# A list schedule that charges TensorE's changes of width, with new plan numbers, in a fused attention and MLP kernel

## Chip, cores and metric

The kernel runs on one core of a Trainium2 chip. What counts is the device time of one execution in microseconds (us).

## The reference

Clustered attention is followed by two MLPs. Queries and keys (2 batches, 8 heads, 768 positions, 64 wide) are each assigned to the nearest of 16 centroids per head, and a query attends to the keys of its own cluster alone. The attention's output, 1536 tokens of 512, goes through two MLPs of 512 to 2048 to 512.

```python
q_assign = np.argmax(np.einsum('bhsd,hcd->bhsc', q_n, c_n), axis=-1)
k_assign = np.argmax(np.einsum('bhsd,hcd->bhsc', k_n, c_n), axis=-1)
mask = q_assign[:, :, :, None] == k_assign[:, :, None, :]
scores = np.where(mask, scale * np.matmul(q, k.transpose(0, 1, 3, 2)), -1000000000.0)
attn = softmax(scores)
x = np.matmul(attn, v)
h = x @ w_in;  x = (h * np.clip(h + 3.0, 0.0, 6.0) / 6.0) @ w_out
h = x @ w_in2; out = softplus(h) @ w_out2
```

(softmax, softplus and the two weight names of the second MLP are written short here.)

## The kernel before, in words

The attention is cut into six blocks (two batches b, three stretches u of 256 queries) of eight heads. For each head and each 128 queries, `chunk` makes the scores in PSUM (L1053), takes the row maximum on VectorE (L1056), the exponential on ScalarE (L1064) and one over the row's sum (L1066 on GpSimd or VectorE, L1068 on VectorE). In the first blocks the weights are transposed by TensorE in fp32 against a diagonal `dg` (L1089) into the one PSUM tile of pool `ps_s3`, and copied to `pt` by VectorE (L1091, four chunks) or ScalarE (L1093). In the others they are split into a high and a low fp16 part (`split`, L544 and L552) and transposed by DMA (L1097). `attend` (L1161 in fp32, L1165 in fp16) multiplies them with v. A head is 64 wide, so these products use half of TensorE's columns; two heads of a pair alternate between the two halves. For one pair that is 36 fp16 products of half width, 18 pairs in all, 648 products. All other fp16 products have the full 128 columns.

Each head's scores need K in two copies: `kb`, and `ka` with 64 rows of K and 16 rows that carry the mask. `prep` (L1018 to L1025) fills ka's lower rows from kb by ScalarE or by DMA, as the plan's `kac` says for each head.

At the start `centroids` (L814 to L850) loads the centroids, transposes them (`c0`, L821), works out their norms on VectorE (L831 to L839), spreads them (`rn`, L844, 16 copies), and transposes the normalised ones (`ct`, L846; copied to `cs`, L850). `first_matrix` (L794 to L806) prepares a matrix for the first mask on GpSimd and VectorE. `assign` multiplies q and k with the centroids (L913), scales on ScalarE, transposes (`at`, L919), and finds the best cluster (L922, L924). For the second batch the assignment products have 32 columns to move (`asc`, L905), twelve to each of four pairs of heads. One-column products (`ams`, L529) add sums over partitions.

The first MLP's products (L735 to L737) run beside the attention from the second block on; the second MLP uses Strassen's scheme (L1465 to L1467, L1630 to L1632). Every fp16 value is a pair (high, low), so three products stand for one.

The order of the work is not the order of the code. The program is first written down in the order of the due times in the table `K`. Then `own_order` builds a graph of all instructions, and `list_schedule` places them, engine by engine, by estimated durations (`estimate`), buffers that come free, and a rank; `justify` goes back from the end and gives new ranks, `K['fb']` times. The resulting order of each engine, of SyncE's DMA issues and of the buffers' turns is then imposed. The planner takes, for an engine, the instruction of best rank among those that can start within `look` ns of the earliest:

```python
            for k in r:
                s = max(free[e], at[k], floor)
...
                if s > least + look:
                    continue
```

Before, `look` is 0 for every engine. For TensorE the planner also keeps its own count of how busy the engine was, and stretches the products when it finds too little (`cold`).

Of the kernel before, what the change touches and what calls it, by code (L numbers as in the profile page):

```python
# [8 lines left out]
F32 = mybir.dt.float32  # L9
# [17 lines left out]
    'qx': -1,  # L27
    'f1': [0],
    'back': 10000,
    'look': {'PE': 0, 'Activation': 0},  # L30
    'pcp': 1,
    'r0p': [1, 2, 3, 4],
    'a0': [-0.829, -0.096, 0.131, 0.512],
    'v0': 0.183,
    'v1': 3.01,
    'a1': [2.168, 2.078, 2.929, 3.267],
    'i': [0.453, 0.631, 0.978, 1.067],
    'il': [0.349, 0.406, 0.323, 0.208],
    'o': [1.182, 1.511, 1.585, 1.881],
    'ol': [0.179, 0.317, 0.272, 0.097],  # L40
    'wd': 0.09,
    'm': [1.41, 2.61, 3.59, 4.703, 6.383],
    'ml': [0.98, 0.767, 1.125, 0.758, 1.25],
    'gq': 3,
    'gr': 1,
    'ahead': 2,
    'lag0': 0.033,
    'lag': 0.23,
    'pl': {},
    'ohb': 2,  # L50
    'gv': 2,
    'gk': [3, 0],
    'gi': [-1, -1, -1],
    'lead': 0,
    'w2o': [1.318, 1.319],
    'ly': [1.051],
    'p4': [0.046, 0.483],
    'p5': [0.833, 0.364],
    'o1': [1.321, 1.068],
    'w2': [0, 0.547, -0.309, 0.875],  # L60
    's2': [6, 13],
    'ly2': [4],
    'mo': [2, 0, 3, 1],
    'P': '',
    'qs': '',
    'x0': [2, 2, 2],
    'f0': [0, 1],
    'ze': [0],
    'w2e': [4.39],
    'w2l': 0.257,  # L70
    'tg': (),
    'we': [(1,), (0,), (0,), (0,)],
    'sb': (2, 2),
    'w2d': 0.176,
    't3': 3.736,
    'w2s': 'left',
    'te': [1, 0, 1, 0, 0, 0, 0, 0, 1, 0, 1, 0, 0, 0, 0, 0],
    'dgb': 2,
    'v2': -1.826,
    'dge': 0,  # L80
    'pg': 1,
    'pk': 1,
# [4 lines left out]
    'qdb': 1,  # L87
    'kbe': [1, 1, 1, 1],
    'dl': 200,
    'fb': 4,  # L90
    'kac': [3, 0],
    'pl_': 100,
    'w2oe': ['dve', 'dve'],
}
P14 = 2.0 ** -14
P26 = 2.0 ** -26
MASK = 2.0 ** 100
# [27 lines left out]
def estimate(op, eng, ins, outs, inst, psum):  # L125
# [8 lines left out]
    if eng == "PE":  # L134
        cols, f32 = elements(ins[0]), str(ins[0].dtype)
        m = inst.tile_size[1]
        if f32 == "dt.float32":
            t = max(cols * m / 76.8, 1.75 * m) + (90 if cols > 256 else 45 if cols > 128 else 5 if m == 128 else 40 if m == 64 else 27)
        else:
            t = cols / 2.4 + (15 if "32r" in f32 else 2.5)  # L140
            if m < 128:
                t = t / 2 + 5
        return t, t + K['pl_'], False
    if eng == "DVE":
        fast = not any(psum(a) for a in ins) and n > 8 and not getattr(inst, "is_scalar_tensor_tensor", False)
        if n <= 4:
            t = 145
        elif op == "Memset":
            t = 100 + n / 1.92
        elif op in ("TensorScalarPtr", "TensorCopy") and fast:  # L150
            t = 150 + n / 1.92
        else:
            t = 146 + n / 0.96
# [3 lines left out]
    if eng == "Activation":  # L157
        if op == "LoadActFuncSet":
            return 1200, 1330, False
        t = 200 + n / 1.2 + 85 * sum(elements(a) == 1 for a in ins[1:]) - (40 if any(psum(a) for a in ins) else 0) + (90 if len(outs) > 1 else 0)  # L160
        return t - 100, t + 30, False
    if eng == "Pool":
        if op == "TensorTensor":
            t = 170 + n * 2.15
        elif op in ("TensorScalarPtr", "TensorCopy"):
            t = 190 + n * 0.9 if n > 8 else 200
        else:
            t = 120 + n * 0.85
# [11 lines left out]
def graph(nc):  # L180
    insts = [i for i in nc.cur_bb.bb.instructions if not type(i).__name__.startswith("BassTile") and i.opcode != "RegisterMove"]
    N = len(insts)
    E = [str(i.engine).split(".")[1] for i in insts]
# [4 lines left out]
    after = [[] for _ in range(N)]  # L188
    needs = [0] * N
# [20 lines left out]
    for k, i in enumerate(insts):  # L210
# [6 lines left out]
        for a in ins + outs:  # L217
            t = a.bass_ap.tensor
            if type(t).__name__ != "Tile" or "DRAM" in str(t.space):
                continue  # L220
            if t.name not in users:
                users[t.name] = []
                g = str(t.cap_key)
# [33 lines left out]
        for x, full in before.items():  # L257
            after[x].append((k, full))
            needs[k] += 1

    g = Graph()
    g.insts, g.E, g.T, g.stream, g.cold, g.tiles, g.after, g.needs = insts, E, T, stream, cold, tiles, after, needs
    g.users, g.group, g.order, g.bufs, g.pool = users, group, order, bufs, pool
    return g


def list_schedule(g, slack, rank=None):
# [5 lines left out]
    N = len(E)  # L273
# [15 lines left out]
    at = [0.0] * N  # L289
    free = dict.fromkeys(ready, 0.0)  # L290
    port = {"DVE": 0.0, "Pool": 0.0}
    queue = 0.0
    edge, work, cold = WINDOW, 0.0, True
    for k in range(N):
        if not needs[k]:
            ready[E[k]].add(k)
# [22 lines left out]
    for _ in range(N):  # L319
        best = None  # L320
        for e, r in ready.items():
            floor = queue - K["back"] if e == "SP" else 0.0
            shared = port["Pool" if e == "DVE" else "DVE"] if e in port else 0.0
            look = K["look"].get(e, 0)
            own, least = [], 1e12
            for k in r:
                s = max(free[e], at[k], floor)
                if T[k][2]:
                    s = max(s, shared)
                if s > least + look:  # L330
                    continue
                w = gate(k)
                if w is None:
                    continue
                s = max(s, w)
                least = min(least, s)
                own.append((k, s))
            if own:
                own = min((max(s, least + look), rank[k], s, k) for k, s in own if s <= least + look)
                if best is None or own[2:] < best:  # L340
                    best = own[2:]
        s, k = best
        e = E[k]
        ready[e].discard(k)
        hold, done, shared = T[k]
        if e == "PE":
            while s >= edge:
                cold, work, edge = work < 0.41 * WINDOW, 0.0, edge + WINDOW
            work += stream[k]
            if cold:  # L350
                hold += g.cold[k]
                done = hold + K['pl_']
# [126 lines left out]
def kernel(ctx: ExitStack, tc: tile.TileContext, qT, kT, v, cen, w1i, w1o, w2i, w2o, out):  # L479
# [333 lines left out]
    def centroids():  # L813
# [28 lines left out]
        for p in range(NP):  # L842
            for r in range(4):
                nc.vector.tensor_copy(out=rn0[32 * r:32 * r + 32, p:p + 1], in_=rn[32 * p:32 * p + 32])  # L844
        ct = ps_a.tile([128, 128], F32, tag="a", name="ct")
        nc.tensor.transpose(out=ct, in_=cd.rearrange("p a d -> p (a d)"), identity=ident)  # L846
        ctv = ct.rearrange("p (n a c) -> p n a c", a=2, c=C)
        for half in range(2):
# [903 lines left out]
```

## Time and profile before

| | |
|---|---|
| median of 3 runs | 745.56 us (744.51 to 746.04) |
| the profiled execution | 746.33 us |
| its span, first to last instruction | 744.5 us |
| TensorE busy | 712.8 us (96%), 6178 records |
| VectorE busy | 614.8 us (83%) |
| ScalarE busy | 545.6 us (73%) |
| GpSimd busy | 103.8 us (14%) |
| mean granted TensorE clock | 0.991 |

The span lies within the execution's time; some 1.8 us are around it. Busy time counts every stretch in which at least one instruction of the engine ran. Matmuls are pipelined, so the distance of two starts says more than the duration of one. An fp32 product leaves two records. In the rows, PE is TensorE, DVE VectorE, ACT ScalarE, POOL GpSimd, SPq SyncE's queue of DMA issues.

### The profile page before, as it was taken

The page shows a single profiled execution, that of the slowest core. Times are in us where ns is not written, and L with a number is a line of the kernel's source. Part 1 is how long each engine was busy: PE and PEld are TensorE (multiplying, and loading weights), DVE is VectorE, ACT ScalarE, POOL GpSimd, SP SyncE. Part 2 cuts the span into 40 slices and gives each one's busy share as a digit, 9 for nine tenths or more (in the row PEclk, how much of TensorE's full clock was granted, in tenths as well). Part 3 has the DMA queues.
Part 4 walks back from the last instruction along what each step waited for, and adds up shares of the span by engine and source line. Part 5 has one row for each costly group of instructions (what it writes and reads, how often), then busy time and mean ns, then how long its engine had stood idle before and what let it go on. Part 6 is the DMA issues. An engine that isn't in the chain of part 4 may idle for free.

```text
span 744.5 us, 15777 instructions
## 1 busy us (share of the span) xinstructions
PE 712.8 (96%) x6178; PEld 592.1 (80%) x6178; DVE 614.8 (83%) x1119; ACT 545.6 (73%) x917; POOL 103.8 (14%) x170
## 2 busy tenths in 40 slices
PE   4998989999899999999999999999999999999997
PEld 1466666777688888888888888888889888888886
DVE  5599898999988868888999884999997999947930
ACT  1379789989799969987988873666886478537831
POOL 6023634311412400011012000000000000000000
PEclk8999999999999899999999999999999999999999
DMA  9394535789999958799998976044332000110001
GB/s 182 105 273 139 198 112 153 171 174 219 247 198 176 157 103 160 133 185 190 189 199 174 194 153 160 29 138 125 122 123 77 15 15 2 57 44 15 1 16 43
DMA packets 167482, 96.15 MB, mean 129 GB/s; under 512 B 129568, under 2 KB 154096, under 8 KB 167408
## 3 DMA queue, kind: packets, MB, share of 16 engines
q1 hardware_dynamic: 167408, 95.15, 55.6%
q8 instruction: 48, 0.79, 0.4%
q14 instruction: 26, 0.21, 0.1%
HBM read 54.95 MB, written 7.86 MB: 84 GB/s over the span
## 4 chain that ended last, share of the span: by engine, by line
PE 64%; DVE 19%; ACT 8%; DMA 3%; issue 3%; POOL 1%; SPq 0%; ACTq 0%; POOLq 0%; DVEq 0%
PE s L1053 6%; PE avt L1165 4%; PE h L1467 4%; PE h L1466 4%; PE h L1465 4%; PE y L735 4%; PE y L737 4%; PE y L736 4%; PE h L735 3%; PE h L736 3%; PE h L737 3%; DVE w L552 3%; PE o L1630 3%; PE o L1631 3%; PE o L1632 3%
## 5 line engine op out<-in xcount | busy, mean ns | idle before, releaser
L1056 DVE TENSOR_REDUCE nm<-s 128x1 f32<-128x768 f32 x96 | 91.2, 953 | 27.9 <-PE s L1053 26.6
L737 PE MATMUL y<-g,w 128*128 128x256 f16 x384 | 105.9, 276 | 0.9 <-DVE w L552 0.8
L735 PE MATMUL y<-g,w 128*128 128x256 f16 x384 | 105.9, 276 | 0.5 <-ACT ys L1248 0.5
L736 PE MATMUL y<-g,w 128*128 128x256 f16 x384 | 105.9, 276 | 0.0
L736 PE MATMUL h<-x,w 128*128 128x256 f16 x384 | 104.8, 273 | 0.9 <-DVE x L552 0.9
L735 PE MATMUL h<-x,w 128*128 128x256 f16 x384 | 104.7, 273 | 0.5 <-ACT pt L1093 0.3
L737 PE MATMUL h<-x,w 128*128 128x256 f16 x384 | 104.7, 273 | 0.0
L1064 ACT ACTIVATE e<-s,nm 128x768 f32<-128x768 f32 x96 | 85.9, 895 | 23.3 <-DVE r L1068 5.0
L1466 PE MATMUL h<-y,w 128*128 128x256 f16 x336 | 90.8, 273 | 0.0
L1465 PE MATMUL h<-y,w 128*128 128x256 f16 x336 | 90.3, 272 | 0.3 <-ACT y L544 0.3
L1467 PE MATMUL h<-y,w 128*128 128x256 f16 x336 | 90.3, 273 | 0.0
L735 PEld LDWEIGHTS <-w 128*128 128x128 f16 x768 | 75.9, 99 | 17.6 <-issue 7.4
L737 PEld LDWEIGHTS <-w 128*128 128x128 f16 x768 | 75.9, 99 | 14.4 <-issue 4.2
L736 PEld LDWEIGHTS <-w 128*128 128x128 f16 x768 | 76.0, 99 | 13.3 <-issue 4.3
L552 DVE SCALAR_TENSOR_TENSOR hl<-e,r,hl 128x768 f16<-128x768 f32 x72 | 74.0, 1032 | 3.3 <-ACT hl L544 2.6
L544 ACT ACTIVATE hl<-e,r 128x768 f16<-128x768 f32 x72 | 66.4, 927 | 3.6 <-DMA pt<-hl 2.2
L552 DVE SCALAR_TENSOR_TENSOR g<-a,sg,g 128x512 f16<-128x512 f32 x72 | 52.2, 759 | 9.0 <-ACT g L544 9.0
L544 ACT ACTIVATE g<-a,sg 128x512 f16<-128x512 f32 x72 | 49.0, 714 | 7.0 <-DVE a L1525 5.5
L1053 PE MATMUL s<-kb,qa 128*128 128x384 f32 x160 | 49.8, 385 | 3.7 <-ACT e L1064 3.7
L1066 POOL TENSOR_SCALAR r<-sm 128x1 f32<-128x1 f32 x64 | 24.8, 388 | 166.8 <-ACT e L1064 165.5
L1089 PEld LDWEIGHTS tr<-dg,e 128*128 128x128 f32 x288 | 35.0, 191 | 16.2 <-issue 10.8
L1228 ACT ACTIVATE r<-h,three,c 128x512 f32<-128x512 f32 x48 | 37.0, 771 | 12.8 <-PE h L737 11.5
(246 smaller groups left out, 1755.7 us busy)
## 6 DMA issues: line engine op xcount, KB each, us to landing
raw<-in_moe_w_out_dram SPq DMA_DIRECT2D x32, 512.0 KB, 3.9
raw<-in_moe_w_in_dram SPq DMA_DIRECT2D x8, 1024.0 KB, 5.2
raw<-in_moe_w_in_dram SPq DMA_DIRECT2D x16, 512.0 KB, 4.8
rk<-in_k_dram SPq DMA_DIRECT2D x12, 384.0 KB, 3.9
ka<-kb SPq DMA_DIRECT2D x20, 192.0 KB, 3.2
st<-in_v_dram SPq DMA_DIRECT2D x12, 256.0 KB, 4.2
ydram<-ys SPq DMA_DIRECT2D x12, 256.0 KB, 2.4
yl<-ydram SPq DMA_DIRECT2D x6, 512.0 KB, 3.9
```

What stands on the lines that cost most here:

```text
L544: nc.scalar.activation(out=hi, in_=src, func=ACTF.Copy, scale=scale)
L552: nc.vector.scalar_tensor_tensor(out=lo, in0=src, scalar=scale, in1=hi, op0=ALU.mult, op1=ALU.subtract)
L735: nc.tensor.matmul(out=ps, lhsT=wt.lhsT(kk, m, 0), rhs=xh, start=start, stop=False)
L736: nc.tensor.matmul(out=ps, lhsT=wt.lhsT(kk, m, 0), rhs=xl, start=False, stop=False)
L737: nc.tensor.matmul(out=ps, lhsT=wt.lhsT(kk, m, 1), rhs=xh, start=False, stop=stop)
L1053: nc.tensor.matmul(out=s[:, n, 0:SH], lhsT=x[:, q], rhs=y[:, n * SH:(n + 1) * SH], start=i == 0, stop=i == len(pairs) - 1)
L1056: nc.vector.tensor_reduce(out=nm, in_=sv, op=ALU.max, axis=AX.XY, negate=True)
L1064: nc.scalar.activation(out=e.rearrange("p (a s) -> p a s", a=2), in_=sv, func=ACTF.Exp, bias=nm, scale=scale, accum_out=sm)
L1228: nc.scalar.activation(out=r, in_=h, func=ACTF.Relu, scale=c1[b][:, j:j + 1], bias=three)
L1465: nc.tensor.matmul(out=ps[:, o, :], lhsT=hi, rhs=y[:, 0, kk], start=first and o == kk == 0, stop=False, skip_group_check=True)
L1466: nc.tensor.matmul(out=ps[:, o, :], lhsT=hi, rhs=y[:, 1, kk], start=False, stop=False, skip_group_check=True)
L1467: nc.tensor.matmul(out=ps[:, o, :], lhsT=lo, rhs=y[:, 0, kk], start=False, stop=kk == 1, skip_group_check=True)
```

## The change

Four things change in the planner. A change between half-width fp16 products and any other product is charged, 95 ns on entering a half-width run and 110 ns on leaving it (`SWITCH`). The estimate of a half-width product falls by 4.5 ns, and a transpose gets its own estimate. `look` becomes 100 ns for TensorE and 60 ns for ScalarE and VectorE. All DMA issues wait in the graph for the first one written, the centroids' load. The table's numbers change with it: due times, `fb` from 4 to 2, and `kac`. One line of the kernel itself changes: `ct` moves from pool `ps_a` (one buffer, which `at` uses next) to `ps_s` (two buffers).

```diff
-    'look': {'PE': 0, 'Activation': 0},
+    'look': {'PE': 100, 'Activation': 60, 'DVE': 60},
...
-    'fb': 4,
-    'kac': [3, 0],
+    'fb': 2,
+    'kac': [0, 0, 0, 1],
...
+SWITCH = (95.0, 110.0)
...
-        if f32 == "dt.float32":
+        if inst.is_transpose:
+            t = 110
+        elif f32 == "dt.float32":
...
             if m < 128:
-                t = t / 2 + 5
+                t = t / 2 + 0.5
...
+    sp = [k for k in range(N) if E[k] == "SP"]
+    for k in sp[1:]:
+        after[sp[0]].append((k, False))
+        needs[k] += 1
...
+    g.part = [E[k] == "PE" and i.tile_size[1] == 64 and "16" in str(i.ins[0].dtype) for k, i in enumerate(insts)]
...
-                s = max(free[e], at[k], floor)
+                s = max(free[e] + (SWITCH[part] if e == "PE" and g.part[k] != part else 0.0), at[k], floor)
...
         if e == "PE":
+            part = g.part[k]
...
-        ct = ps_a.tile([128, 128], F32, tag="a", name="ct")
+        ct = ps_s.tile([128, 128], F32, tag="s", name="ct")
```

The numbers that move due times (`a0`, `v0`, `o1`, `w2` and others, 16 of them in all) stand in the table and tell a reader nothing by themselves; what they do is seen in the order.

The same instructions stand in both programs, but for the copies of ka's lower rows: 20 by ScalarE and 20 by DMA before; 30 by ScalarE, 10 by GpSimd (every fourth head) and none by DMA now. On SyncE the centroids' load, second before, is now first, and the q load that was first is second; the next twelve loads are the same.

On TensorE, in the second block, the third pair of heads, the first with fp16 weights, is multiplied with v (`avt`; pt_1480 and pt_1627 are its two heads' weights, `ams` is a one-column sum). Before:

```order
L1165 LDWEIGHTS v_442
L1165 MATMUL avt_1977<-pt_1480,v_442 64x256
L529 MATMUL ams_1843<-wss_1447,one_s_77 128x1
L1165 LDWEIGHTS v_442
L1165 MATMUL avt_1977<-pt_1627,v_442 64x256
L1165 LDWEIGHTS v_442
L1165 MATMUL avt_1977<-pt_1480,v_442 64x256
```

Now, at the beginning of the same pair's products:

```order
L1176 LDWEIGHTS v_415
L1176 MATMUL avt_1970<-pt_1480,v_415 64x256
L746 LDWEIGHTS w_1141
L746 MATMUL y_1877<-g_1787,w_1141 128x256
L540 MATMUL ams_1843<-wss_1444,one_s_77 128x1
L1176 LDWEIGHTS v_415
L1176 MATMUL avt_1970<-pt_1627,v_415 64x256
L1176 LDWEIGHTS v_415
```

Before, the one-column sum cut the pair's products into runs of 4 and 31 behind a first lone one; now the sum stands ahead of a run of 35, and the first product is still alone.

On VectorE, the copy of the transposed weights of the first block's sixth head (`pt_754`), for which TensorE's next transpose waits. Before:

```order
L552 SCALAR_TENSOR_TENSOR w_590<-st_591,w1i_s_81,w_590 128x1024
L1201 TENSOR_SCALAR c1_0_736<-w1i_i_82,vs0_462 128x1
L552 SCALAR_TENSOR_TENSOR v_441<-st_456,vs0_462,v_441 128x2x128
L552 SCALAR_TENSOR_TENSOR w_590<-st_591,w1i_s_81,w_590 128x1024
L1091 COPY pt_754<-tr_757 128x6x128
L552 SCALAR_TENSOR_TENSOR x_501<-avt_502,vs0_462,x_501 128x2x256
```

Now:

```order
L563 SCALAR_TENSOR_TENSOR x_501<-avt_502,vs0_435,x_501 128x2x256
L1067 TENSOR_REDUCE nm_871<-s_868 128x1
L1071 TENSOR_SCALAR nm_871<-nm_871 128x1
L1077 TENSOR_SCALAR r0_835<-sm_833 128x1
L1079 RECIPROCAL r_837<-r0_835 128x1
L1067 TENSOR_REDUCE nm_906<-s_903 128x1
L1102 COPY pt_754<-tr_757 128x6x128
```

The weights' splits (w_590) have moved ahead, out of the copy's way; row maxima of the following heads' scores now stand there.

On TensorE, the fourth pair's assignment products of the second batch (asc_3470 before, asc_3419 now). Before:

```order
L905 MATMUL asc_3470<-cs_155,rq_3466 128x32 x2
L529 MATMUL ams_3159<-vam_3141,one_s_77 128x1
L905 MATMUL asc_3470<-cs_155,rq_3466 128x32 x4
L905 MATMUL asc_3470<-cs_155,rk_3468 128x32
L735 LDWEIGHTS w_1141
L735 MATMUL y_3113<-g_3073,w_1141 128x256
L905 MATMUL asc_3470<-cs_155,rk_3468 128x32 x3
L1053 MATMUL s_3327<-kb_2928,qa_2784 128x384 x2
L1053 MATMUL s_3327<-ka_2927,qa_2784 128x384 x2
L905 MATMUL asc_3470<-cs_155,rk_3468 128x32
```

Now:

```order
L916 MATMUL asc_3419<-cs_155,rq_3415 128x32 x6
L916 MATMUL asc_3419<-cs_155,rk_3417 128x32
L746 LDWEIGHTS w_1141
L746 MATMUL y_3113<-g_3110,w_1141 128x256
L916 MATMUL asc_3419<-cs_155,rk_3417 128x32 x2
L1064 MATMUL s_3276<-kb_2928,qa_2784 128x384 x2
L1064 MATMUL s_3276<-ka_2927,qa_2784 128x384 x2
L916 MATMUL asc_3419<-cs_155,rk_3417 128x32
```

The one-column sums have left the group, and two of its twelve products now come some 50 full-width products later.

## Rows read from the trace of the kernel before

**Rows 1.** Page, engines: busy us, share of the span, instructions.

```profile
PE 712.8 (96%) x6178; PEld 592.1 (80%) x6178; DVE 614.8 (83%) x1119; ACT 545.6 (73%) x917; POOL 103.8 (14%) x170
```

**Rows 2.** Stretches: from:to, length, busy (records) by engine, clock, DMA share, GB/s.

```profile
80.00:120.00 40.00, 34.97 (x226) 24.95 (x225) 38.49 (x72) 33.74 (x64) 18.80 (x28) 1.00 0.50 155
...
160.00:200.00 40.00, 35.54 (x325) 28.33 (x323) 39.94 (x79) 33.26 (x56) 8.90 (x15) 1.00 1.03 237
200.00:300.00 100.00, 98.83 (x881) 82.56 (x882) 80.88 (x151) 91.22 (x162) 20.38 (x29) 0.97 0.86 158
```

**Rows 3.** TensorE's waits: us in total, times, longest.

```profile
PE s L1053 <- ACT e L1064: 4.1, 6, 1.4
...
PE tr L1089 <- ACT pt L1093: 2.6, 2, 1.4
```

**Rows 4.** Timeline from 299 to 304: start, length, engine, line.

```profile
299.82 0.27 PE L735 MATMUL h<-x,w 128*128 128x256 f16 x1
...
299.93 0.27 PE L736 MATMUL h<-x,w 128*128 128x256 f16 x1
...
300.41 2.05 PE L1165 MATMUL avt<-pt,v 128*64 128x256 f16 x34
...
303.03 0.28 PE L735 MATMUL y<-g,w 128*128 128x256 f16 x1
...
303.24 0.30 PE L1165 MATMUL avt<-pt,v 128*64 128x256 f16 x1
...
303.47 0.28 PE L736 MATMUL y<-g,w 128*128 128x256 f16 x1
```

**Rows 5.** Timeline of the start.

```profile
0.73 0.75 SPq L885 DMA_DIRECT2D q<-in_q_dram  x1
...
1.54 0.58 SPq L817 DMA_DIRECT2D cw<-in_centroids_dram  x1
1.54 1.48 DVE L780 CAST identb<-ident 128x128 bf16<-128x128 f32 x1 [0.15 <-POOL ident masks.py:199]
1.57 1.37 POOL L879 MEMSET q<- 64x1536 f32 x1
...
4.87 0.23 DVE L796 CAST fw<-fw 128x128 f32<-128x128 int32 x1 [1.85 <-POOL fw L794]
...
5.80 0.39 PE L821 MATMUL c<-ident,cw 128*64 128x128 f32 x1 [5.80 <-DMA cw<-in_centroids_dram]
...
12.89 0.46 DVE L850 COPY cs<-ct 64x64 f32<-64x64 f32 x2
...
13.49 0.56 PE L919 MATMUL at<-ident,sa 128*128 128x128 f32 x3 [2.85 <-DVE cs L850]
14.10 0.56 DVE L922 TENSOR_REDUCE mx<-at 128x24 f32<-128x384 f32 x1 [0.75 <-PE at L919]
```

**Rows 6.** DMA issues, first 45 us, then whole span: KB each, us to landing.

```profile
k<-oh SPq DMA_DIRECT2D x2, 24.0 KB, 1.8
...
ka<-kb SPq DMA_DIRECT2D x20, 192.0 KB, 3.2
```

**Rows 7.** Timeline around 72 us.

```profile
71.53 1.27 DVE L552 SCALAR_TENSOR_TENSOR w<-st,w1i_s,w 128x1024 f16<-128x1024 f32 x1
...
72.73 0.95 DVE L1091 COPY pt<-tr 128x768 f32<-128x768 f32 x1
...
73.82 0.68 PE L1089 MATMUL tr<-dg,e 128*128 128x128 f32 x4 [2.31 <-DVE pt L1091]
```

**Rows 8.** Groups by line: busy us, mean ns, idle before and its releaser.

```profile
L1018 ACT ACTIVATE ka<-kb 64x768 fp32r<-64x768 f32 x20 | 16.9, 843 | 5.9 <-PE s L1053 5.6
```

**Rows 9.** Stretch at the low clock, columns as in rows 2.

```profile
252.78:259.60 6.82, 6.82 (x31) 4.98 (x31) 6.73 (x15) 6.72 (x15) 1.24 (x3) 0.50 0.88 112
```

**Rows 10.** Timeline of TensorE from 180 to 189.

```profile
181.21 1.43 PE L905 MATMUL asc<-cs,rq 128*128 128x32 f32 x12
182.48 1.50 PE L905 MATMUL asc<-cs,rk 128*128 128x32 f32 x12
```

More of the change, by code (lines that the diff above doesn't have):

```diff
@@ L29 @@
     'back': 10000,
-    'look': {'PE': 0, 'Activation': 0},
+    'look': {'PE': 100, 'Activation': 60, 'DVE': 60},
     'pcp': 1,
     'r0p': [1, 2, 3, 4],
-    'a0': [-0.829, -0.096, 0.131, 0.512],
-    'v0': 0.183,
-    'v1': 3.01,
+    'a0': [-0.859, -0.096, 0.103, 0.512],
+    'v0': 0.104,
+    'v1': 3.333,
     'a1': [2.168, 2.078, 2.929, 3.267],
@@ L39 @@
     'o': [1.182, 1.511, 1.585, 1.881],
-    'ol': [0.179, 0.317, 0.272, 0.097],
+    'ol': [0.179, 0.317, 0.253, 0.097],
     'wd': 0.09,
-    'm': [1.41, 2.61, 3.59, 4.703, 6.383],
-    'ml': [0.98, 0.767, 1.125, 0.758, 1.25],
+    'm': [1.395, 2.61, 3.59, 4.703, 6.383],
+    'ml': [0.98, 0.767, 1.125, 0.66, 1.25],
     'gq': 3,
@@ L46 @@
     'ahead': 2,
-    'lag0': 0.033,
-    'lag': 0.23,
+    'lag0': 0.027,
+    'lag': 0.213,
     'pl': {},
@@ L54 @@
     'lead': 0,
-    'w2o': [1.318, 1.319],
-    'ly': [1.051],
-    'p4': [0.046, 0.483],
+    'w2o': [1.374, 1.445],
+    'ly': [1.18],
+    'p4': [-0.044, 0.759],
     'p5': [0.833, 0.364],
-    'o1': [1.321, 1.068],
-    'w2': [0, 0.547, -0.309, 0.875],
+    'o1': [1.464, 1.035],
+    'w2': [0, 0.283, -0.244, 0.875],
     's2': [6, 13],
-    'ly2': [4],
+    'ly2': [0],
     'mo': [2, 0, 3, 1],
@@ L68 @@
     'ze': [0],
-    'w2e': [4.39],
+    'w2e': [4.136],
     'w2l': 0.257,
@@ L73 @@
     'sb': (2, 2),
-    'w2d': 0.176,
-    't3': 3.736,
+    'w2d': 0.194,
+    't3': 4.036,
     'w2s': 'left',
@@ L78 @@
     'dgb': 2,
-    'v2': -1.826,
+    'v2': -1.856,
     'dge': 0,
@@ L293, in list_schedule @@
     edge, work, cold = WINDOW, 0.0, True
+    part = False
     for k in range(N):
```

## The prediction, made before the changed kernel was run

> **What bounds the kernel now.** I read the page first: TensorE is busy 712.8 us, 96% of the span of 744.5 [rows 1], so at most some 32 us are waits, and the rest shrinks only if TensorE's own work gets cheaper. The stretches then say where the 32 us lie: 5 us of the 40 from 80 to 120 and 4.5 of the 40 from 160 to 200 are idle, but only 1.2 of the 100 from 200 to 300 [rows 2]. In those two idle stretches VectorE is busy 38.49 and 39.94 us of 40, so VectorE, not TensorE, is the limit there. The waits name the places: TensorE waits for ScalarE's exponentials (4.1 us) and for copies of the transposes (2.6 us on ScalarE) [rows 3]. The reader should see three kinds of loss: waits before 200 us, TensorE time lost at changes of form, and time lost to a lower clock.
>
> **Changes of form (gain).** In a run of full-width fp16 products one starts 0.11 us after the last (299.82, 299.93). In a run of half-width products 34 take 2.05 us, 0.06 us each, since the two halves of the array work side by side. Where one half-width product stands alone between full-width ones, the starts are 303.03, 303.24 and 303.47: 0.21 us in and 0.23 us out, 0.44 where 0.11 + 0.06 would do [rows 4]. So a lone product costs 0.27 us too much, and a run of any length pays 0.10 on entering and 0.12 on leaving, 0.22 in all. Counted in the two orders, the 648 half-width fp16 products stand in 44 runs before and 34 after; 19 of the 44 are lone, 16 of the 34. Three lone ones fewer give 3 x 0.27 = 0.8 us, seven other runs fewer 7 x 0.22 = 1.5 us: **2.3 us**. Bounds: 0, where TensorE would have waited there anyway, and 2.3. I take 2.2, because most of these runs stand among the MLP's products, where TensorE hardly waits (1.2 us of the 100 from 200 to 300 [rows 2]), so that the cost is on the path; one of the runs may fall where it waits anyway. That 16 lone ones stay is not a failure of the change: the first product of a pair goes early, and its partner's tile comes later.
>
> **The start (gain).** Centroids are issued second, at 1.54, behind a q load at 0.73, and the product that needs them starts at 5.80, 4.2 us later [rows 5]. Issued first, they start 0.81 us earlier. A transfer of 24 KB on a nearly empty queue lands in 1.8 us [rows 6], where these 32 KB took 4.2; so the landing comes 0.81 to 0.81 + 2.4 = 3.2 us sooner. I take 1.4, nearer to the lower end, whose row is the transfer itself. The pool move lets the transposes at 13.49 run without waiting for the two copies of ct at 12.89 (2.85 us of idle). But the reduce that reads them stands behind those copies on VectorE in both orders, so what is saved is only the time from the copies' end, 13.35, to the reduce at 14.10, 0.7 us [rows 5]. Against this stands VectorE's own order: eight of the nine steps that prepare the first mask ran ahead of the centroids' norm or between its steps, and all nine now come behind it. At the 0.23 us of the one at 4.87 eight cost 1.8 us; below it is 0, if the norm's steps, each waiting for the last, leave as much room elsewhere. I take 1.4 (an estimate, near the end that the row gives). Sum 1.4 + 0.7 - 1.4: **0.7 us**, bounds 0 and 2.5. From there on everything hangs on this chain, since the first scores, the v loads and the paced weights all start from it.
>
> **Waits before 200 us (gain).** The longest is at 71.51: TensorE has nothing but a transpose whose PSUM tile is still to be copied, and the copy stands on VectorE behind a weight split of 1.27 us (71.53). It starts at 72.73, and TensorE goes on at 73.82, after 2.31 us [rows 7]. In the new order no split stands ahead of that copy: a score's maximum does, and TensorE has one attention product, two score products and two one-column products between. What is left is at most the copy itself, 0.95 us, less 1.1 us of those products, or a maximum of 0.96 that comes first: **1.5 us** gained. Of the other 11 us I cannot say from an order which go; VectorE's work in 160 to 200 is the same and was full. For them I take 0, with 3 us either way.
>
> **K's lower half (ka).** 20 transfers ka<-kb of 192 KB vanish, their copies go 10 to ScalarE and 10 to GpSimd. ScalarE pays 10 x 0.84 = 8.4 us [rows 8], beside TensorE: it is busy 91 of 100 us in 200 to 300 while TensorE idles 1.2. Cost 0 as long as that slack (9%) takes it; the bound is the whole 8.4. SyncE loses 20 issues, each of which landed 3.2 us after its issue [rows 6], so nothing becomes later there; I count no gain, as TensorE's long waits name other things [rows 3]. Queued behind a GpSimd copy is the scale of a chunk's sum on the same engine, which the reciprocal waits for.
>
> **The clock.** TensorE runs at 1.2 instead of 2.4 GHz from 252.78 to 259.60 (granted 0.50), having run tiny assignment products in a row before; at half rate 6.82 us do the work of 3.41, so this costs **3.4 us** [rows 9]. The same sort of row, 24 records in 2.77 us from 181.21 on [rows 10], drew no such stretch (the 40 us from 160 to 200 ran at 1.00 [rows 2]). So a row of these products can lower the clock, but need not. In the new order the fourth group is thinner (two of its twelve go 50 full-width products later, and no one-column products stand in it), the third is split around a run of half-width products, but the first and the second stand as twelve in a row. I expect one such stretch somewhere, as before: **0**, with 3.4 either way. By the Trainium skill (TensorE: Matmul & The Clock Gate, part 1) the chip's window is free-running and doesn't reset when a kernel starts, so that the planner, which counts from its own zero, could not place these groups safely. The one execution traced agrees in so far as one of four like groups was hit; by that rule the term would be a chance and not a gain.
>
> **The sum.** 2.2 + 0.7 + 1.5 = 4.4 us, and the clock the same. The profiled execution took 746.33, of which 744.5 is the span and 1.8 lies around it; less 4.4 this is 741.9. It lies 0.8 above the median of the three timed runs, 745.56, so against that I say **741.2**. All of its own bounds, without the clock: 739 to 743.5.
>
> **Rivals.**
> - No low-clock stretch after the start, 741.2 - 3.4 = **737.8**. For it: the fourth group is thinned and the third split. Against it: two groups of twelve stand whole.
> - The gain goes to a second stretch at the low clock, or to new waits of that size, 741.2 + 3.4 = **744.6**. For it: every engine's order before 200 us is shuffled at once, and two whole groups remain. Against it: one group in four was hit.
> - Slower, by the GpSimd copies of ka. A cast on VectorE of 128x128 took 1.48 us beside a GpSimd memset of 1.37 (both near 1.55), and one of the same size 0.23 at 4.87 [rows 5], so one GpSimd pass can hold VectorE 1.25 us. Ten copies could hold it 12.5 us. Some four of them lie between 80 and 200 us, where VectorE is full, the rest later, where it has some to spare (19% from 200 to 300 [rows 2]). Six on the path cost 7.5: **748.7**. From the fifth (5 x 1.25 = 6.3, more than the 4.4 gained and the 1.5 that count as no change) the kernel is slower. Against it: GpSimd is busy 14% of the span as it is [rows 1], and ten copies add little to that. The Trainium skill (GPSIMD Engine Reference, Specifications) says GpSimd shares its SBUF interfaces with VectorE, and contention comes with VectorE instructions that use two ports or two SBUF inputs; by that, these copies would be felt in the two-input splits too, which are VectorE's largest share. The rows here show it for the cast alone.
>
> **Chances.** The forecast 0.38, no low stretch 0.18, gain given back 0.24, slower 0.20. Some 1.5 us (0.2% of 745.56) is what a measurement of this kernel can tell from no change: 744.07 to 747.05. Faster by more: nearly all of the first, the second, and a good third of the third case, 0.63; within: 0.17; slower: 0.20. The range takes in 737.8 with some of its spread, and leaves out the most of the GpSimd case: 737.0 to 747.5.
>
> **What would show it.** Right: 34 runs of half-width products, entries and exits still near 0.21 and 0.23; centroids landing near 4.3 us, the first row maximum before 13.5; no wait over 1 us at the transpose after VectorE's fourth copy of one; one stretch at 1.2 GHz past 130 us. Wrong: entries and exits that cost the same with TensorE's idle time larger before 200 us; two or no low-clock stretches; VectorE instructions beside the ka copies longer than before, or ScalarE with no idle time between 200 and 300 us and TensorE waiting for it.

## The result and the profile after

The changed kernel takes **737.92 us** (median of 6 runs, 736.93 to 738.91) against 745.80 (744.51 to 749.02, 6 runs): ratio 0.9888, 95% interval [0.9865, 0.9910], 7.9 us faster. The forecast was 741.2 with a range of 737.0 to 747.5, so the direction held and the time lies inside the range, but 3.3 us below the forecast and below the bounds of its own case (739 to 743.5). A second set of runs of the same kernel gave 739.26 (737.11 to 743.89, 7 runs) against 746.21, ratio 0.9919 [0.9886, 0.9953], 7.0 us faster.

The page of the profiled execution (736.93 us) answers to [rows 1]; the columns are the same.

```profile
PE 705.1 (96%) x6178; PEld 592.3 (81%) x6178; DVE 619.9 (84%) x1119; ACT 552.9 (75%) x927; POOL 113.8 (15%) x180
```

The span is 735.1 us against 744.5. TensorE's busy time fell by 7.7 us and its idle time (span less busy) from 31.7 to 30.0. So most of what was won in these two executions is not a wait that went. A good part of it is the clock: the execution traced before had a second stretch at the low clock (granted 0.50), in the start, beside the one at 252.78 of [rows 9] (columns as there):

```profile
13.84:20.67 6.83, 4.96 (x22) 1.57 (x22) 3.08 (x5) 0.49 (x1) 0.00 (x0) 0.50 0.80 169
```

TensorE was busy for 4.96 and 6.82 us in the two, and for 3.41 us in the only one of the change's first execution (172.53, below). Half of the difference, 4.2 us of the 7.7, is an estimate of what the clock did to the busy time of these two profiles. So the profiles alone can't tell what the new order is worth.

The stretches answer to [rows 2]; the last is one that the trace shows at the low clock.

```profile
80.00:120.00 40.00, 36.01 (x240) 26.62 (x240) 39.02 (x67) 34.92 (x63) 16.85 (x27) 1.00 0.46 152
160.00:200.00 40.00, 36.19 (x315) 29.87 (x314) 37.32 (x78) 35.98 (x62) 10.23 (x13) 0.96 0.91 206
200.00:300.00 100.00, 98.42 (x922) 83.81 (x920) 85.43 (x149) 94.41 (x165) 23.34 (x35) 1.00 0.78 154
172.53:175.94 3.41, 3.41 (x18) 2.72 (x18) 3.41 (x7) 3.41 (x6) 0.83 (x1) 0.50 1.02 274
```

VectorE is still nearly full from 80 to 120 (39.02 of 40), and TensorE idles 4.0 and 3.8 us in the two stretches where it idled 5.0 and 4.5. ScalarE has nine copies of ka in 200 to 300 where it had six (94.41 us busy against 91.22), and TensorE idles 1.6 there. The low-clock stretch at 252.78 of [rows 9] has no counterpart in this execution; one of half its length lies at 172.53.

The start answers to [rows 5]: SyncE's issues, then VectorE, then TensorE, in three pieces of the timeline.

```profile
0.73 0.39 SPq L828 DMA_DIRECT2D cw<-in_centroids_dram  x1
1.18 0.76 SPq L896 DMA_DIRECT2D q<-in_q_dram  x1
...
2.54 0.39 PE L832 MATMUL c<-ident,cw 128*64 128x128 f32 x1 [2.54 <-DMA cw<-in_centroids_dram]
2.97 0.35 DVE L835 COPY cs<-c 64x64 f32<-64x64 f32 x2
4.11 0.16 DVE L850 RECIPROCAL rn<-n 128x1 f32<-128x1 f32 x1
4.77 0.23 DVE L807 CAST fw<-fw 128x128 f32<-128x128 int32 x1 [0.50 <-POOL fw L805]
...
10.37 0.55 PE L930 MATMUL at<-ident,sa 128*128 128x128 f32 x3 [0.41 <-ACT sa L926]
11.14 0.46 DVE L861 COPY cs<-ct 64x64 f32<-64x64 f32 x2
11.63 0.56 DVE L933 TENSOR_REDUCE mx<-at 128x24 f32<-128x384 f32 x1
```

The centroids' product starts 1.8 us after its load's issue, at 2.54 instead of 5.80. The whole norm chain (2.97 to 4.27) is done before the first mask cast can start at 4.77, since that one waits for GpSimd. The transposes `at` start before the copies of ct, and the first row maximum stands right behind these copies, at 11.63 instead of 14.10: **2.5 us earlier**. Of the norm's lead (done at 4.27 instead of 8.56) only 1.75 us reach the copies of ct, 11.14 instead of 12.89, because the mask's steps now stand between.

The waits of TensorE, the longest first, answer to [rows 3]: in total, times, longest.

```profile
PE tr L1100 <- ACT pt L1104: 3.8, 6, 1.1
PE asc L924 <- DVE fw L808: 2.9, 1, 2.9
PE c L832 <- DMA cw<-in_centroids_dram: 2.5, 1, 2.5
PE s L1064 <- ACT e L1075: 2.4, 6, 0.6
PE et L944 <- DVE eq L935: 2.4, 2, 1.9
PE tr L1100 <- POOL dg L1089: 2.0, 1, 2.0
PE y L748 <- DVE w L563: 1.8, 1, 1.8
```

The wait of 2.31 us of [rows 7] is gone. In its place stand two of 0.5 (the timeline of TensorE around 70 us):

```profile
69.86 1.13 PE L1100 MATMUL tr<-dg,e 128*128 128x128 f32 x8 [0.53 <-ACT pt L1104]
...
71.50 1.24 PE L1064 MATMUL s<-k,q 128*128 128x384 f32 x3 [0.52 <-ACT e L1075]
```

But new ones have come: 2.0 for a diagonal from GpSimd at 100, 1.8 for a weight split at 161.

Half-width products, as in [rows 4] (timeline of TensorE from 300):

```profile
300.68 0.28 PE L746 MATMUL h<-x,w 128*128 128x256 f16 x1
300.89 2.15 PE L1176 MATMUL avt<-pt,v 128*64 128x256 f16 x35
302.98 0.28 PE L747 MATMUL h<-x,w 128*128 128x256 f16 x1
303.09 0.27 PE L748 MATMUL h<-x,w 128*128 128x256 f16 x1
```

Entering a run still takes 0.21 us (300.68 to 300.89), and leaving it 0.21 to 0.23 as before (here from 302.77, the start of the run's last product, to 302.98); there are 34 runs, 16 of them lone products, as counted.

### The profile page after: what moved, and what is told of

Same layout as the page of the kernel before. It is cut to its first block, busy times and chain, and to the rows that moved or that the text cites. A ratio compares the mean times of both kernels' runs of the same rounds, so it can differ in the third digit from the quotient of the medians.

```text
span 735.1 us, 15820 instructions
## 1 busy us (share of the span) xinstructions
PE 705.1 (96%) x6178; PEld 592.3 (81%) x6178; DVE 619.9 (84%) x1119; ACT 552.9 (75%) x927; POOL 113.8 (15%) x180
## 3 DMA queue, kind: packets, MB, share of 16 engines
q1 hardware_dynamic: 165808, 91.22, 52.3%
## 4 chain that ended last, share of the span: by engine, by line
PE 62%; ACT 5%; DVE 4%; issue 2%; DMA 1%; POOL 0%; ACTq 0%
PE h L1476 5%; PE h L1478 5%; PE h L1477 5%; PE y L746 5%; PE y L747 5%; PE y L748 5%; PE s L1064 4%; PE avt L1176 3%; PE h L746 3%; PE h L747 3%; PE h L748 3%; PE o L1641 3%; PE o L1643 3%; PE o L1642 3%; PE y L1606 2%
## 5 line engine op out<-in xcount | busy, mean ns | idle before, releaser
L1077 POOL TENSOR_SCALAR r<-sm 128x1 f32<-128x1 f32 x64 | 26.3, 411 | 160.7 <-ACT e L1075 158.3
L1100 PE MATMUL tr<-dg,e 128*128 128x128 f32 x288 | 40.8, 283 | 6.5 <-ACT pt L1104 3.8
```

Source lines behind the costliest of these rows:

```text
L1100: nc.tensor.matmul(out=tr[:, kt, :], lhsT=e[:, (k0 + kt) * 128:(k0 + kt + 1) * 128], rhs=dg, start=True, stop=True)
```

## The experiments

All twelve kernels were compared with the kernel before on the same chip. Where one is compared with the change at a given place of the order, both traces hold the same products there, and the difference of their starts is called its lag.

**1 to 4: the change again, lone products joined, long runs cut, the start undone.** `e1_after` is the change itself.

> The changed kernel again, to stand beside its edits on one chip. If the gain is the order's (start, width changes, waits), it is 7 to 9 us faster than the kernel before whatever the mean granted clock of a run. If the gain is the low-clock stretch that the profiled execution of the kernel before had from 252.78 to 259.60 and that of the changed one had not, runs of the changed kernel with a mean clock of 0.991 to 0.993 should be about 3.4 us slower than one with 0.998.

Measured: 739.26, given above. In the first set the runs with a mean granted clock of 0.991 to 0.993 took 737.5 to 738.9 us, 0.6 to 2.0 more than the one with 0.998, not 3.4. So the gain is the order's for the most part, by the expectation's own measure. The execution profiled here took 743.89, 7 us more than the one profiled first, from the same program. Of the 7 us, 1.3 lie around the span (3.1 in place of 1.8). Three stretches at the low clock explain most of the rest:

```profile
104.13:114.37 10.24, 9.88 (x38) 7.28 (x37) 9.11 (x18) 8.99 (x17) 5.38 (x8) 0.50 0.62 201
175.81:182.64 6.83, 6.83 (x36) 4.76 (x35) 6.83 (x13) 5.15 (x10) 1.13 (x2) 0.50 1.05 283
15.38:18.79 3.41, 3.34 (x15) 1.04 (x6) 1.97 (x3) 0.58 (x1) 0.00 (x0) 0.50 1.06 197
```

Against the first execution it lags 1.0 us at 100, 3.6 at 120 and 5.1 at 180, and never makes it up. Which of these stretches come differs between executions of one program.

`e2_join` moves each lone half-width product of the change to the next run of the same tile:

```diff
+        for (a, b), (c, _) in zip(r, r[1:]):
+            if b - a == 1 and q[a] not in done and set(g.tiles[q[a]]) & set(g.tiles[q[c]]):
+                break
...
+        new = q[:a] + q[b:c] + [k] + q[c:]
```

> The changed kernel with its order kept, but each of the 16 lone half-width products moved behind to its own run: 18 runs in place of 34. If changes of width are on the path: 16 x 0.27 = 4.3 us faster than the changed kernel, near 733.6. If TensorE's waits take such savings back: 0 to 1 us faster, near 737.5; waiting longer with the first product of a run could even cost.

Measured: 736.37 (734.96 to 740.66, 4 runs), ratio 0.9882 [0.9843, 0.9922]. That is 2.9 below e1_after, but the intervals overlap. The lag against the change's first profile is cleaner: it falls from 4.5 us at 260 to 2.9 at 480, where no low-clock stretch lies in either. In that part 10 runs are gone: 0.17 each.

`e3_split` cuts 18 long runs by one full-width product after the 18th.

```diff
+        for x in range(b, b + 12):
+            k = q[x]
...
+            m = a + 18
+            new = q[:m] + [k] + q[m:x] + q[x + 1:]
```

> The changed kernel with its order kept, but one full-width product from behind each of the 18 long half-width runs put into its middle: 52 runs in place of 34. If changes of width are on the path: 18 x 0.22 = 4.0 us slower than the changed kernel, near 741.9. If the cost falls where TensorE would wait anyway: 0 to 1 us slower.

Measured: 747.74 (10 runs), ratio 1.0013 [0.9991, 1.0036]: 8.5 us above e1_after, twice what was expected. In the profile the lag grows by 1.8 us from 260 to 500, where 12 runs were added, 0.15 each. 7 us come at once around 250: a wait of 2.5 us for ScalarE's g at 248.56, and behind it a low-clock stretch of 10.24 us from 252.12. So a run costs 0.15 to 0.17 us in this order, and the greater part of this edit's cost is another one: a wait, and the clock behind it.

`e4_q_first` keeps the change's whole order and puts the first q load ahead of the centroids again.

```diff
+    q = queues["SP"]
+    q[0], q[1] = q[1], q[0]
```

> The changed kernel with its order kept, but the first q load issued before the centroids, as before. The centroids should land about 3 us later (first product near 5.8 instead of 2.5) and VectorE's first row maximum come 2 to 3 us later. If the start is on the path to the end: 2 to 3 us slower than the changed kernel, near 740.5. If later limits take it back (the lead over the kernel before fell from 5.3 us at 20 to 2.9 at 70): 0 to 1 us slower.

Measured: 743.28 (10 runs), ratio 0.9960 [0.9943, 0.9977]: **4.0 us above e1_after** by medians, 3.1 by ratios. Its first row maximum stands on VectorE at 15.01:

```profile
6.10 0.35 DVE L876 COPY cs<-c 64x64 f32<-64x64 f32 x2 [3.03 <-PE c L873]
7.23 0.16 DVE L891 RECIPROCAL rn<-n 128x1 f32<-128x1 f32 x1
7.31 0.38 DVE L848 CAST fw<-fw 128x128 f32<-128x128 int32 x1
...
15.01 0.56 DVE L974 TENSOR_REDUCE mx<-at 128x24 f32<-128x384 f32 x1
```

The maximum is 3.4 us later than in the change, and 0.9 later than before. The lag against the change's first profile is 4.8 us at 20, 3.8 at 100 and 3.7 at 300 and 480. e1_after, which also had a low-clock stretch in the start, lags 1.0 at 100, so up to 2.8 us are the late load's; up to, because this execution's stretch (6.83 us) was twice as long as that one's (3.41). From 100 us on nothing of it is made up.

**5 and 12: the start alone, in the order of before.** `e5_before_cfirst` has the same exchange of two loads in the kernel before and nothing else.

> The kernel before with one edit: on SyncE's queue the centroids' load and the first q load change places, everything else in the order of before. The trace of the change put the centroids' transposes 3.3 us earlier and the first row maximum 2.5 us earlier, and the run with the q load put back ahead of the centroids lost 3.8 to 4.8 us that it never got back. Theory 'the start carries through': 3 to 4 us below the kernel before, ratio near 0.995. Rival 'the start is absorbed, it was worth something only in the order planned for it': within 1 us of before, ratio 0.999 to 1.001, with an idle stretch of TensorE before 60 us that is 2 to 3 us longer than before's.

Measured: 746.25 (12 runs), ratio 0.9990 [0.9975, 1.0006]: nothing. The theory fell at its first step, since the first row maximum didn't move (13.97). VectorE's order shows why:

```profile
4.88 0.23 DVE L798 CAST fw<-fw 128x128 f32<-128x128 int32 x1 [1.85 <-POOL fw L796]
...
8.32 0.15 DVE L841 RECIPROCAL rn<-n 128x1 f32<-128x1 f32 x1
...
13.97 0.56 DVE L924 TENSOR_REDUCE mx<-at 128x24 f32<-128x384 f32 x1 [0.70 <-PE at L921]
```

The centroids are there at 2.5, but the mask cast stands ahead of them and waits for GpSimd, and the norm is done at 8.5, not at 4.3. `e12_before_start` therefore also gives VectorE's operations of the start the order that the change gives them.

```diff
+    order = [9, 11, 13, 15, 17, 19, 21, 7, 25, 26, 27, 28, 8, 10, 23, 12, 14, 16, 24, 18, 31, 20, 32, 22, 33, 29, 30, *range(34, 43)]
+    new = q[:7] + [q[x] for x in order] + q[43:]
```

> The kernel before with the centroids' load first, as in the run that gained 0 to 1 us by it, and VectorE's first 47 operations in the order that the change gives them: the seven steps on the centroids' norm and copies stand ahead of the first mask cast, which waits for GpSimd until 4.8, and the rn copies are spread between the mask steps; nothing else moves. Theory 'the load pays only together with VectorE's order, and then carries': the first row maximum at 11.6 to 12.7 in place of 13.97, 1.3 to 2.4 us, and the time 1.5 to 3.7 us below before, ratio 0.995 to 0.998. Rival 'the head start is used up by later waits in the order of before, planned for a late start': the first row maximum as early, the time within 1 us of before, ratio 0.999 to 1.001.

Measured: 744.16 (12 runs) against 746.36, ratio 0.9972 [0.9954, 0.9989]: 2.2 us faster. On VectorE:

```profile
3.04 0.35 DVE L870 COPY cs<-c 64x64 f32<-64x64 f32 x2
4.17 0.16 DVE L885 RECIPROCAL rn<-n 128x1 f32<-128x1 f32 x1
4.87 0.23 DVE L842 CAST fw<-fw 128x128 f32<-128x128 int32 x1 [0.54 <-POOL fw L840]
...
11.63 0.46 DVE L896 COPY cs<-ct 64x64 f32<-64x64 f32 x2
12.79 0.56 DVE L968 TENSOR_REDUCE mx<-at 128x24 f32<-128x384 f32 x1 [0.70 <-PE at L965]
```

So the load and VectorE's order pay only together: the first row maximum stands at 14.10 before, 13.97 with the load alone, 15.01 with the order and the late load (in the change), 12.79 with both. The 0.70 us between the copies' end and the maximum, which the pool move takes away, is still there; in the change VectorE also reaches the copies half a microsecond sooner (11.14). For 1.3 us won at the maximum the whole kernel got 2.2, with an interval of 0.8 to 3.4. The profiles don't show how: against the profile of before the lead is 1.3 us at 20, 0.8 at 40 and 0.4 from 70 to 240, as the rival has it. Then it jumps to 3.2 between 253 and 260, where the profile of before has its low-clock stretch and this one has none. Over all runs the mean clock of the two kernels is the same (0.9885 and 0.9888), so the 2.2 us are not the clock's on the mean; how much of the head start carries in the order of before stays open.

**6 and 7: the rules without the numbers, the numbers without the charge.** `e6_rules` is the change with the number table of before; `e7_nosw` is the change with the charge at zero. Both are planned anew.

```diff
-    'fb': 2,
-    'kac': [0, 0, 0, 1],
+    'fb': 4,
+    'kac': [3, 0],
...
```

> The rules of the change (centroids first, the charge for a change of width, runs kept whole) with the number table of the kernel before, planned anew; the ka copies are then all DMAs as before. It has 31 runs of half-width products against 44 before and 34 in the change. Theory 'the rules make the gain': start -3.7, 13 runs fewer at 0.22 each -2.9, so 6 to 7 us below before, near the changed kernel, ratio 0.990 to 0.993. Rival 'the new numbers make the gain, the rules alone leave new waits': 0 to 3 us below before, ratio 0.996 to 1.000.

```diff
-SWITCH = (95.0, 110.0)
+SWITCH = (0.0, 0.0)
```

> The change with its charge for a change of width set to zero and planned anew: 47 runs of half-width products in place of 34, 19 of them lone in place of 16; centroids first, numbers as in the change. Theory 'each run costs its entry and exit, about 0.22': 13 times 0.22 is 2.9 us slower than the change, ratio against before 0.992 to 0.994. Rival 'the width changes hide in waits': within 1 us of the change, ratio 0.988 to 0.990. If the whole gain came from the width rule: back at before, ratio 0.998 to 1.001.

Measured: e6_rules 751.39 (12 runs), ratio 1.0053 [1.0029, 1.0076], slower than before; e7_nosw 748.54 (12 runs), ratio 1.0014 [0.9995, 1.0032], the whole gain lost. For e6_rules neither theory had this; e7_nosw came out at its last case, "the whole gain", but not for the reason given there, as its trace shows. Both kernels have the early start: at 20 us they lead the kernel before by nearly 4 us. (Here the orders differ, and the lead is taken where TensorE has begun the same number of records.) TensorE's waits in e6_rules:

```profile
PE tr L1100 <- ACT pt L1104: 2.9, 2, 2.4
PE ams L540 <- ACT pt L1104: 2.9, 1, 2.9
...
PE avt L1176 <- DMA pt<-hl: 1.9, 1, 1.9
```

It idles 35.7 us (span 749.9 less 714.2 busy) against the change's 30.0. Its executions also have a lower clock, 0.984 on the mean against 0.987 of before on the same chip, so part of the loss may be the clock's. In e7_nosw the lead over before is 9.2 us at 360 (the change's is 7.7), 5.5 at 480 and 0.2 at 500. There TensorE waits twice for a g split of the MLP (2.6 us in all) and runs at the low clock from 492.07:

```profile
PE y L747 <- DVE g L563: 2.6, 2, 1.6
```

```profile
492.07:495.48 3.41, 2.94 (x14) 2.07 (x14) 3.41 (x6) 0.80 (x2) 0.00 (x0) 0.50 0.00 0
```

So the charge's worth is not 13 runs at 0.22. A changed rule gives another plan everywhere, and the numbers fit only the rules that they were set for. What each rule would be worth with numbers of its own was not tried.

**8: GpSimd's copies of ka.** `e8_nopool` makes the ten GpSimd copies DMAs again and keeps every other order.

```diff
-            nc.gpsimd.tensor_copy(out=ka[0:64], in_=kb[here].bitcast(F32))
+            nc.sync.dma_start(out=ka[0:64].bitcast(F32), in_=kb[here].bitcast(F32))
```

> The change with its ten GpSimd copies of kb into ka made DMAs on SyncE's queue, as all twenty were before; every other instruction of TensorE, VectorE and ScalarE stands as in the change. Theory 'the copies cost nothing, VectorE's hl split was 1049 ns on the mean with them and 1032 without': within 1 us of the change, ratio 0.987 to 0.991. Rival 'GpSimd's copies hold VectorE up': 2 us or more faster than the change, ratio below 0.986. Rival 'the copies save a late ka': 2 us or more slower, with waits of TensorE for ka at the scores.

Measured: 738.56 (6 runs), ratio 0.9891 [0.9863, 0.9918], the same as the change. VectorE's hl split, first in the change, then here (72 of them, mean ns behind the busy time):

```profile
L563 DVE SCALAR_TENSOR_TENSOR hl<-e,r,hl 128x768 f16<-128x768 f32 x72 | 75.4, 1049 | 6.8 <-ACT hl L555 6.3
```

```profile
L586 DVE SCALAR_TENSOR_TENSOR hl<-e,r,hl 128x768 f16<-128x768 f32 x72 | 73.6, 1023 | 7.6 <-ACT hl L578 7.2
```

The 26 ns are not the copies' doing, though: in the change only five of the 72 splits run beside a ka copy, four of them for 0.03 us. What such a copy does is seen at the fifth:

```profile
311.86 0.82 POOL L1031 CAST ka<-kb 64x768 fp32r<-64x768 f32 x1 [0.73 <-POOL raw L523]
312.19 1.30 DVE L563 SCALAR_TENSOR_TENSOR hl<-e,r,hl 128x768 f16<-128x768 f32 x1
```

This split took 1.30 us, where the splits beside no GpSimd instruction take 1.01 on the mean. Two other instructions with two inputs in SBUF overlap a copy for 0.49 and 0.76 us and are 0.35 and 0.63 us longer than their like; row maxima beside a copy take 0.95 us as elsewhere. That makes 1.3 us of VectorE's time over the whole span, and the time of the kernel is the same without it.

**9 and 10: taking away the waits that are left.** `e9_waits` turns the order at four places where the change still waits, four waits of TensorE at 100, 104, 161 and 167 to 169 us.

```diff
+        ("DVE", [194, 191, 192, 193], "r,r0"),
+        ("DVE", [305, 308, 306, 307, 311, 312, 309, 310], "nm,s"),
+        ("Pool", [66, 65], "dg,ident,r"),
+        ("Activation", [94, 96, 92, 93, 95], "pt,tr1"),
+        ("PE", [710, 711, 712, 713, 709], "y,g,w"),
+        ("PE", [715, 716, 717, 718, 719, 720, 721, 722, 723, 724, 714], "asc,cs,rq"),
```

> The change with four places of its order turned by hand where TensorE still waits: VectorE's reciprocal and GpSimd's diagonal go ahead of the row maximum and the scale they stood behind (1.97 us wait at 100.05 of the change's profile), ScalarE's two pt copies ahead of two weight casts (1.13 at 104.20), VectorE's splits of w ahead of an hl split (1.79 at 161.55), and TensorE's two amax products behind four y products and ten second-batch score products (0.48 at 167.50 and 1.03 at 168.82). Theory 'a wait that nothing else replaces is worth its length to the end': the first, second and fourth go, the third falls to 0.3 to 0.8, together 5 us: 4 to 6 us below the change, ratio against before 0.981 to 0.985. Rival 'waits are given back, the next operand is late instead': 0 to 1.5 us below the change, ratio 0.987 to 0.990, with the idle time between 100 and 175 us of the profile as long as before (7.9 us) at other places.

Measured: 740.68 (6 runs), ratio 0.9913 [0.9883, 0.9943]: no gain. The waits that were taken out went, and others came (waits of TensorE):

```profile
PE s L1117 <- ACT e L1128: 3.8, 8, 1.2
...
PE et L994 <- DVE eq L988: 2.5, 1, 2.5
...
PE avt L1225 <- DVE x L616: 2.0, 1, 2.0
```

At 104 the diagonal is in time, and now the product behind the transposes waits 2.0 us for x on VectorE. At 177 TensorE waits 2.5 us for the next cluster maximum, which stands on VectorE behind an hl split. From 50 to 200 us TensorE is busy 137.46 us against 138.19 in the change:

```profile
50.00:200.00 150.00, 137.46 (x1027) 105.84 (x1020) 140.18 (x275) 132.78 (x233) 52.99 (x77) 0.98 0.63 164
```

So TensorE's idle time in this stretch is 12.5 us, not less than the change's 11.8. (From 100 to 175 us, the part named above, it is 5.7 against 7.4; the new wait at 177 lies behind.) The rival is borne out, the waits are handed on. VectorE is busy 140 to 143 of these 150 us before, in the change and here, and its work did not shrink; that this is the reason is argued, as no run shortened it.

`e10_best` takes these edits, the joins of e2_join, and the first row maximum moved ahead of three copies.

> All edits that promise a gain on the change together: the four places of the run on waits, the 16 lone half-width products joined to their neighbours (18 runs in place of 34), and the first row maximum moved ahead of three copies on VectorE. If they add: waits -5, joins -1.5 to -2.9 as that run's profile gave, first maximum -0.3 to -0.6, so 7 to 8 us below the change, 729 to 731, ratio 0.977 to 0.980. If the waits are given back: 735 to 737, ratio 0.986 to 0.988.

Measured: 739.61 (6 runs), ratio 0.9898 [0.9864, 0.9933]. No version beats the change by more than the measurement can tell.

**11: the joins alone, in the order of before.** The edit of e2_join in the kernel before, 28 runs in place of 44.

> The kernel before with one edit on TensorE's order alone: lone half-width products moved to the next run of the same tile, so 28 runs in place of 44 and 1 lone product in place of 19; no other engine's order moves and the loads stand as before. Theory 'each run costs 0.22 to 0.27 for entry and exit, in any order': 16 fewer, 3.5 to 4.3 us below before, ratio 0.994 to 0.995. Rival by the same edit on the change (1.5 to 2.9 for 16): ratio 0.996 to 0.998. Rival 'the widths cost nothing that a wait does not hide': within 1 us, ratio 0.999 to 1.001.

Measured: 748.45 (12 runs), ratio 1.0018 [0.9998, 1.0037]: no gain, at a mean clock of 0.984 against 0.987 of before on this chip. From 320 to 480 of before's order 8 runs are gone and the lag falls by 2.7 us, 0.34 each. But ahead of it ScalarE stands still for 6.69 us:

```profile
302.20 0.94 ACT L600 ACTIVATE hl<-e,r 128x768 f16<-128x768 f32 x1 [6.69 <-DMA pt<-hl]
```

A lone product, once joined, comes later, so its pt tile comes free later. The next DMA transpose was issued at 297.24, right behind a lone product moved to 296.91, and until it was done hl was held; TensorE waited 3.8 us for the exponential behind it, and a low-clock stretch of 6.83 us followed at 302.83. That the moved product was what held the transpose is read from the times; it wasn't tried by itself. In the order of the change the same joins brought no such wait.

## Why the prediction was right, and where it was off

The direction and the range were right. The gain was 7.0 to 7.9 us by the medians of the two sets, where 4.4 was forecast. The term that was most off is the start.

**The start was mis-sized** by its landing. The centroids landed 3.3 us earlier, not 1.4: that is the far bound (0.81 + 2.4), since a transfer first in the queue landed as fast as the 24 KB one of [rows 6], 1.8 us after its issue. The pool move gave its 0.7. The 1.4 us set against them, for the mask's steps behind the norm, was nearly right: 3.3 + 0.7 less the 2.5 us that arrive at the first row maximum leaves 1.5. It comes about otherwise than argued. The first mask step can't begin before GpSimd is done at 4.8 (the 1.85 us of idle time ahead of the cast in [rows 5]), and the norm, run through in that gap, wins 1.0 us more than the landing gave; then the mask's steps take 2.5 of the lead. So the term is 2.5 us where 0.7 was forecast. What 2.5 us at the maximum are worth at the end is an estimate: in the order of the change 3.4 us there cost 3.1 to 4.0 of time (e4_q_first, by the ratios and by the medians), which makes 2.2 to 3.0. That everything hangs on this chain holds in the order of the change; in the order of before 0.4 of 1.3 us were left by 70 us (e12_before_start).

**Changes of form** were nearly right: 10 runs fewer at the 0.15 to 0.17 us of e3_split and e2_join are 1.5 to 1.7 us, where 2.2 was forecast. In the order of before the price was 0.34 in the part where it could be read. But the change's rule cannot be judged by this price, as e7_nosw and e11_before_join show.

**Waits before 200 us:** the one at 71.51 went as argued, but the sum did not shrink by 1.5. From 50 to 200 us TensorE idles 12.8 us before and 11.8 after (first before, then after):

```profile
50.00:200.00 150.00, 137.21 (x1035) 103.49 (x1034) 140.97 (x279) 131.69 (x232) 51.21 (x75) 1.00 0.69 184
```

```profile
50.00:200.00 150.00, 138.19 (x1041) 107.58 (x1041) 143.28 (x281) 134.98 (x235) 53.68 (x77) 0.99 0.63 166
```

That a wait is worth its length was the weak step, and e9_waits refutes it for this stretch.

**ka** at 0 was right, and the rival "slower, by GpSimd's copies" falls with e8_nopool. It had the mechanism but not the size: it put 1.25 us on a copy and six copies on the path. Where a copy ran beside an instruction with two inputs in SBUF for 0.49 us or more, that one took 0.3 to 0.6 us longer, and only three of the ten copies did so. The Trainium skill (GPSIMD Engine Reference, Specifications) expects contention with VectorE instructions that have two SBUF inputs; the trace agrees, with 1.30 us in place of 1.01 for such a split, and no change for the row maxima, whose one input is in PSUM.

**The clock** was put at 0, either way 3.4. The price of the stretch at 252.78 was nearly right: e5_before_cfirst and e12_before_start have TensorE's order of before and no stretch there, and both gain 2.8 to 3.1 us on it between 253 and 260. But "one such stretch, as before" left out that the execution traced before had two, the other one in the start. The time of 737.9 is that of the rival "no low-clock stretch after the start". That is luck, since its mechanism did not come: both profiles of the change have such stretches, one in the first, two in the second (and a third in its start), which took 743.89. Over all executions whose clock is on record its mean is 0.9879 before (85) and 0.9916 with the change (13). What is missing to full speed is then 9.0 and 6.2 us of a span. So the clock gave at most 2.8 us. Along a line through the executions of before, 1 us so lost is worth 0.4 us of time, which makes it 1.1; along one through the change's 13, 0.8. That it is the orders that make the clock fall more or less often is argued, not shown. By the Trainium skill (TensorE: Matmul & The Clock Gate, part 1) the chip's window is free-running; the trace fits that, in that one program had one stretch in one execution and three in another.

**The sum** by the runs: start 2.2 to 3.0, forms 1.5 to 1.7, waits 1.0, clock 1.1 to 2.8, together 5.8 to 8.5, against 7.0 and 7.9 measured. The start's and the clock's shares overlap in the runs that they are read from, and how much of the last two belongs to which rule stays open.

## What to carry to other kernels

A load that comes earlier is worth what its consumer's engine makes of it: read what stands ahead of the consumer on its queue and what that waits for, and move both or neither. Where one engine is full over a stretch, moving operations ahead of a wait can just hand the wait on, as it did here; to shorten that engine's work would be the next thing to try. In a planned order the price of one transition doesn't price the rule, since a rule and the plan's numbers are one setting.

## What was not expected of the hardware

- The same program took 736.93 and 743.89 us in two executions, with 3.41 us at the low clock in the one and 20.48 in the other.
- Most low-clock stretches of all the profiles, 34 of 44, begin near four places, 12 to 15, 103 to 111, 171 to 180 and 249 to 255 us, but which of them come differs by execution. In the change's first profile the one at 172.53 began while 12 assignment products of 32 columns (24 records, from 170.09) ran in a row, and none came behind the group near 245.
- Ahead of the stretch at 252.78 of the kernel before TensorE had been busy without a break from 245.90 on (6.88 of 6.88 us).
- Interrupting a long run of half-width products costs 0.15 us net, less than its entry and exit read from single starts (0.10 and 0.12 over).
